# A hand-planned attention and long-convolution kernel: new starting rules for GpSimd, new due times for loads, and a new placement of the exponentials on VectorE

## The chip, the cores and the metric

The kernel runs on one core of a Trainium2 chip. The metric is the device time of one execution in microseconds (us), lower is better.

## The reference

```
x = A_q                                    # [1, 2048, 640], bf16
g = sigmoid((x * gate_w).sum(-1))          # one gate for each token
# A: a shift convolution of 4 taps along time, then a convolution of full length
k_shift[t] = sum_j A_k[t - j] * shift_k[:, j]
kv = k_shift * A_v
y  = irfft(rfft(pad(kv)) * rfft(pad(ssm_k)))[:2048] + kv * ssm_D
a  = x * y
# B: attention, 32 heads of 20 columns for the queries, one shared head for keys and values
q = (x @ wq) in 32 heads;  k = x @ wk;  v = x @ wv          # k, v: [2048, 20]
p = softmax(q @ k.T * 20 ** -0.5)          # 32 x 2048 x 2048
b = (p @ v, heads side by side) @ wo
out = g * a + (1 - g) * b
```

## The kernel before

**Attention is the main work.** The 32 heads by 2048 queries are cut into 32 groups of 4 heads (rows r = 0 to 3 of TensorE) by 512 queries, called G, and the 2048 keys into 16 steps, called j. One (G, j, r) is a tile of 128 keys by 512 queries, 2048 tiles in all. For each tile TensorE makes the scores in PSUM (`score`, L1310), an engine takes the exponential and writes bf16, and TensorE multiplies by the values and adds in PSUM bank 6 (`PVmm`, L1400). At a group's end VectorE copies the sums to `acc` (L1474), a round trip through DRAM (`den`, `rcp`, `rbc`) spreads the reciprocals of the sums, and GpSimd multiplies (`onorm`, L1486).

**Two engines take exponentials.** ScalarE takes most tiles, in units of alternately three tiles (ETA, 1536 columns) and two (ETB, 1024 columns). The table `DVE_J` lists for every group G the steps j in which two of the four tiles go to VectorE instead; this document calls such a two a pair. For a pair VectorE reads two banks of PSUM (dW, L1380, 512 columns each) and then runs three instructions of 1024 columns on SBUF alone (dX twice, L1392 and L1393, and ETd, L1395), a polynomial that gives the bits of the exponential.

**Side work fills the gaps.** The shift convolution (L1632), the long convolution as products with cosine and sine tables (`spectra` L1689, the complex product `mac` L1722 on GpSimd, `inverse` L1757), the projections of later queries (L1217) and the output projection (L1787) have priorities and run on TensorE where the attention leaves room. GpSimd's product of one chunk is five instructions; its inputs X and K have three buffers each. Fillers (L1843, L1848) are matmuls on zeros that keep TensorE busy.

**A planner in the kernel writes the order.** Every operation is an `Op` with an engine, dependencies, a priority and a cost in us. `Scheduler.run` always lets the engine with the earliest clock choose (`pick`), places the operation (`place`), and sets when its successors are ready from its planned end and a latency. A transfer's planned end comes from its bytes, the queue's planned rate and its `lat`. `emit` then writes each engine's list as it stands, with semaphore waits for the dependencies: each engine's order is fixed, and an engine waits where the plan was too early. `port=True` marks VectorE operations that the planner keeps apart from GpSimd's (`port_until`, `pool_until`); reads of PSUM, as dW, are not marked. `pool_may` decides whether GpSimd may begin at its time t, by what VectorE does then: x is the last operation placed on VectorE.

**The head and the loads.** `loads` fetches x in four blocks of 512 tokens (the first in two halves, called xnh), weights, and a slice of wq. `xT` transposes x on TensorE (L1075), with copies to SBUF on VectorE or ScalarE; `kproj` makes keys, values and the bound that the exponentials need; `qproj` projects the queries of groups 0 and 1 and sends a row `cr` of their norms by a small transfer (`qT<-cr`) into the queries, without which no score of that group can be made. `kshift` loads k with four transposing transfers (L1615) and v with four plain ones, on SyncE's queue, in which the q stores (`scr_q`), the q loads and `qT<-cr` stand too. `self.crow0` is the small transfer of group 0; the writer of `("qT0", 1, 4)` is that of group 1.

Of the kernel before, what the change touches and what calls it, by code (L numbers as in the profile page):

```python
# [37 lines left out]
OLD = 6.0  # L38
YOUNG = 4.0
WAITN = 0.5  # L40
HOLD = 0.1
IDLE = 0.3
WAITP = 6.0
PVB = 2
# [127 lines left out]
class Scheduler:  # L172
# [114 lines left out]
    def pool_may(self, t):  # L287
        d = self.order["dve"]
        if not d or not HOLD:
            return True  # L290
        x = d[-1]
        if not x.port and x.end > t + HOLD:
            return True
        if x.end <= t and not any(o.port and o.ready <= t + IDLE for o in self.cand["dve"]):
            return True
        w = [o.ready + (WAITP if o.name != "onorm" else WAITN) for o in self.cand["pool"] if o.ready <= t]
        return bool(w) and t > min(w)
# [175 lines left out]
    def place(self, op, e):  # L473
        t = self.t[e]
        op.eng = e
        if e == "pe":
            mode = MODE.get(op.name, "f")
            if mode != self.mode:
                t += SWITCH
                self.mode = mode  # L480
        if op.alts:
            for x in op.alts:
                self.cand[x].discard(op)
            op.fn, op.cost = op.alts[e]
        else:
            self.cand[e].discard(op)
        if op.main and e == "pe":
            for b in op.banks or ():
                if not self.bank_claimed[b]:
                    self.bank_claimed[b] = True  # L490
                    op.deps.update(self.bank_last[b])
        start = max(t, op.ready)
        if op.kind == "d":
            if op.nbytes:
                begin = max(start + 0.1, self.dma_bw)
                self.dma_bw = begin + op.nbytes / 300e3
                op.end = max(self.dma_bw, start + op.iss) + op.lat
            else:
                op.end = start + op.iss + op.lat
            self.t[e] = start + op.iss  # L500
            best = min(range(NLANES), key=lambda l: self.lanes[l][-1].end if self.lanes[l] else -1.0)
            op.lane = best
            if self.lanes[best]:
                op.deps.add(self.lanes[best][-1])
            self.lanes[best].append(op)
            op.value = 16 * len(self.lanes[best])
        else:
            if op.port and e == "dve":
                op.end = max(start, self.pool_until - PORTP) + op.cost
                self.port_until = op.end  # L510
            elif e == "pool":
                op.end = max(start, self.port_until - PORTD) + op.cost
                self.pool_until = op.end
            else:
                op.end = start + op.cost
            self.t[e] = op.end
        op.start = start
        op.placed = True
        if e == "pe" and op.cost > 0.05:
            self.active.append((op.end - op.cost * 0.92, op.end))  # L520
        if e == "pe":
            if op.name != "qk":
                self.rows = set()
            elif op.cont:
                self.rows.add(op.row)
            else:
                self.rows = {op.row}
        if op.name in ("tp0", "tp1"):
            b = STAGES[int(op.name[2])][2]
            self.bank_claimed[b] = self.bank_busy[b] = False  # L530
            self.bank_last[b] = [op]
            self.bank_ready[b] = op.end + LATX
        if op.name == "pv":
            if op.stage is not None:
                self.filler = self.filler2[op.stage]
            self.can_fill = not op.last
            self.acc = None
        elif op.name == "acc":
            self.acc = op
        if e == "pool" and self.main_started and HOLD:  # L540
            d = self.order["dve"]
            if len(d) > 1 and d[-1].end > t and not d[-1].port:
                op.deps.add(d[-2])
        self.order[e].append(op)
        self.linear.append(op)
        gr = op.grp
        if gr is not None:
            if e == "pe" and op in gr.mms:
                gr.pos += 1
                if gr.pos == len(gr.mms) and self.open is gr:  # L550
                    self.open = None
            elif op in gr.evacs:
                if all(x.placed for x in gr.evacs):
                    b = gr.bank
                    self.bank_busy[b] = False
                    self.bank_last[b] = [gr.mms[-1]] + list(gr.evacs)
                    self.bank_ready[b] = max(x.end + (LATX if self.main_started else LATS[x.eng, "pe"]) for x in gr.evacs)
        for s in op.succ:
            s.nun -= 1
            lat = 0.0 if (s.eng == "pe" and e == "pe") else self.lat_of(op, e, s.eng)  # L560
            s.ready = max(s.ready, op.end + lat)
            sg = s.grp
            if sg is not None and s.eng == "pe" and not (op.grp is sg):
                sg.nun -= 1
                sg.ready = max(sg.ready, op.end + lat)
                if sg.nun == 0:
                    self.gcand.add(sg)
            if s.nun == 0:
                self.enable(s)
# [73 lines left out]
NSC, NDC, NB = 16, 5, 4  # L643
# [16 lines left out]
PORTP = 0.05  # L660
PORTD = 0.14
PORTW = 0.2
INB = ()
LASTG = 31
STAGES = ((0, 256, 6), (256, 128, 5), (384, 128, 6))
DVE_J = ((), (3,), (4, 6, 11, 14), (3, 8, 14), (1, 2, 5, 10), (7, 12, 13), (3, 11), (2, 9, 10, 12), (1, 4, 7, 11, 12, 14), (1, 12), (2, 4, 8, 10, 14), (2, 7, 11), (1, 6, 9, 13), (5, 8, 13, 14), (6, 8, 13), (1, 3, 10, 13, 14), (12,), (2, 9, 14), (2, 8, 9, 13), (1, 8, 9, 13), (2, 4, 6, 11, 12, 14), (1, 8, 11, 12), (), (1, 8, 11, 13, 14), (2, 6, 10, 13, 14), (7, 14), (1, 3, 6, 9, 12), (6, 11, 14), (4, 7, 12), (1, 7, 10), (1, 4, 6, 8, 10, 12, 14), (3, 5))
SCALE = float(DH) ** -0.5


# [32 lines left out]
class Kernel:  # L702
# [171 lines left out]
    def loads(self):  # L874
        T, aps = self.T, self.aps
        x = aps["A_q"][0].rearrange("(i p) d -> p i d", p=128)
        wq = aps["B_wq"].rearrange("(p dc) n -> p dc n", dc=NDC)
        for b in range(NB):
            for lo, hi in ((0, 2), (2, 4)) if b == 0 else ((0, 4),):
                xl = self.dma(T["xn"][:, 4 * b + lo:4 * b + hi, :], x[:, 4 * b + lo:4 * b + hi, :],  # L880
                              writes=[("xn", b) if b else ("xnh", lo)], nbytes=110000 * (hi - lo),
                              prio=-9 + b + 0.1 * lo, lat=6.0)
            if b == 0:
                self.dma(T["wq"][:, :, 0:80], wq[:, :, 0:80], writes=[("wqst", 0)], prio=-8.5, lat=5.0)
        self.xl = [xl]
        for n, w, pr in (("wkr", "B_wk", -98.8), ("wvr", "B_wv", -98.7)):
            self.dma(T[n][:, :, :], aps[w].rearrange("(p dc) c -> p dc c", dc=NDC), writes=[n], eng="act",
                     prio=pr, lat=4.5)
        self.dma(T["gwr"][:, :], aps["gate_w"].rearrange("(p dc) -> p dc", dc=NDC), writes=["gwr"],
                 eng="act", prio=-98.6, lat=5.5)  # L890
        self.dma(T["wq"][:, :, 80:640], wq[:, :, 80:640], writes=[("wqst", 1)], nbytes=716800, prio=-4,
                 after=self.xl)
        self.dve(lambda e: e.memset(T["Drow"][:, :], 0.0), (), ["Drow"], 0.4, prio=-990)
# [169 lines left out]
    def xT(self):  # L1063

        T = self.T
# [1 line left out]
        plan += [(b, 0, 4, d0, min(2, NDC - d0)) for b in range(1, NB - 1) for d0 in range(0, NDC, 2)]  # L1067
        plan += [(NB - 1, c, 1, 0, NDC) for c in range(4)]
        for b, c0, nc, d0, nd in plan:
            gr = self.group("xT", 0.5 + 0.1 * b, banks=(0, 1, 2, 3, 4, 5, 7))  # L1070
            n = 128 * nc
            for dc in range(d0, d0 + nd):
                for ci in range(nc):
# [531 lines left out]
    def kshift(self):  # L1605
# [4 lines left out]
        self.dma(T["wtap"][:, :, :], self.aps["A_shift_k"].rearrange("(c p) j -> p c j", p=128), writes=["wtap"],  # L1610
                 nbytes=5120, prio=3, after=self.crow0, lat=3.0)
        self.dve(lambda e: e.memset(T["kTr"][:, :, 12:16], 0.0), (), [("kTr", -1)], 0.2, prio=20, after=self.crow0)
        for b in range(NB):
            o, i = T["kTr"][:, :, 16 + 512 * b:528 + 512 * b], k[512 * b:512 * b + 512, :]
            x = self.g.add("sp", lambda e, o=o, i=i: e.dma_start_transpose(o, i), (), [("kTr", b)], 0.1, kind="d",  # L1615
                           nbytes=655360, prio=14 + b, lat=1.6, after=self.crow0, name="ld_k")
            x.iss = 3.3
            self.dma(T["kv"][:, 4 * b:4 * b + 4, :], v[:, 4 * b:4 * b + 4, :], writes=[("kvl", b)], nbytes=655360,
                     prio=14.5 + b, name="ld_v", after=self.crow0)
        sh = [128, NDC * 4, 128]  # L1620
        self.dve(lambda e: e.tensor_tensor(
            T["kdiag"][:, :, :, :].rearrange("p c j d -> p (c j) d"), T["ident"][:, :].unsqueeze(1).to_broadcast(sh),
# [280 lines left out]
```

## Time and profile before

| What | Value |
|---|---|
| median of three runs (lowest, highest) | 862.49 us (861.33, 862.59) |
| the profiled execution: its own time | 861.71 us |
| its span on the core, first to last instruction | 859.9 us |
| ScalarE busy | 841.7 us |
| VectorE busy | 788.3 us |
| TensorE busy (fillers among it) | 836.1 us |
| GpSimd busy | 378.1 us |
| first exponential of the attention begins at | 20.63 us |
| last one begins at | 852.98 us, takes 1.45 us |

The span is what the profile's times count from. Busy times are unions of an engine's instructions; a share of busy time says little by itself here, since TensorE runs fillers and VectorE's instructions include the time that they stand locked. Groups of instructions are given by line, engine and operation, as "out<-in", with their count, busy time, mean duration in ns of one, and the idle time of their engine just ahead of them. SPq is SyncE's queue. The chain of waits is read back from the last instruction: at each step what released it.

### The profile page before, as it was taken

The numbers are of one execution on the slowest core, as the hardware profiler recorded it, in microseconds if no ns is written. First come the engines' busy times: TensorE is split into PE (matmuls) and PEld (weight loads), VectorE is DVE, ScalarE is ACT, GpSimd is POOL, SyncE is SP. The second block draws the span as 40 slices with busy tenths as digits, with TensorE's granted clock in tenths as the row PEclk, the third lists the DMA queues.
The fourth block names the chain that finished last, engine by engine and source line by source line (L and its number), as shares of the span: only waits on it lengthen the run. The fifth ranks groups of instructions, "written<-read, shape, count | busy, mean of one in ns | idle before, by whom it ended". The sixth has DMA issues, their size and how long they took to land.

```text
span 859.9 us, 18774 instructions
## 1 busy us (share of the span) xinstructions
PE 836.1 (97%) x8073; PEld 349.3 (41%) x8073; DVE 788.3 (92%) x968; ACT 841.7 (98%) x753; POOL 378.1 (44%) x317
## 2 busy tenths in 40 slices
PE   8999999999999999999999999999999999999998
PEld 5244433443344444444334434444343344433334
DVE  7679999999989999999999989999999988889995
ACT  6989999999999999999999999999999999999997
POOL 3656104566444356553317754335666565000000
PEclk9999999999999999999999999999999999999999
DMA  6910130002110000100120101100200001312111
GB/s 177 270 55 8 39 87 22 14 13 52 47 44 20 14 8 27 38 20 20 31 60 14 45 21 42 30 14 14 44 20 21 15 2 45 82 31 64 39 38 40
DMA packets 55765, 36.31 MB, mean 42 GB/s; under 512 B 33057, under 2 KB 51714, under 8 KB 55682
## 3 DMA queue, kind: packets, MB, share of 16 engines
q1 hardware_dynamic: 55106, 34.90, 15.0%
q8 instruction: 63, 1.03, 0.5%
q10 hardware_dynamic: 576, 0.22, 0.1%
q14 instruction: 20, 0.16, 0.1%
HBM read 20.31 MB, written 8.51 MB: 34 GB/s over the span
## 4 chain that ended last, share of the span: by engine, by line
ACT 78%; PE 17%; DVE 4%; DMA 0%; issue 0%; POOL 0%; POOLq 0%
ACT ETA L1347 47%; ACT ETB L1347 32%; PE ps L1310 5%; PE ps L1689 3%; PE ps L1400 3%; PE ps L1757 2%; PE ps L1843 1%; PE ps L1848 1%; DVE dW L1380 1%; DVE dX L1392 1%; PE ps L1511 1%; PE ps L1217 1%; DVE dX L1393 1%; PE ps L1075 0%; DMA qT<-cr 0%; DVE ETd L1395 0%
## 5 line engine op out<-in xcount | busy, mean ns | idle before, releaser
L1347 ACT ACTIVATE ETA<-ps 128x1536 bf16<-128x1536 f32 x366 | 579.6, 1584 | 5.6 <-PE ps L1310 5.4
L1347 ACT ACTIVATE ETB<-ps 128x1024 bf16<-128x1024 f32 x365 | 424.5, 1163 | 0.0
L1310 PE MATMUL ps<-qT,kT 32*128 32x512 bf16 (+2 forms) x2176 | 302.9, 372 | 14.6 <-ACT ETA L1347 7.2
L1722 POOL TENSOR_TENSOR Pp<-X,K 128x1024 f32<-128x1024 bf16 (+1 forms) x80 | 145.3, 1824 | 140.6 <-DVE K L1710 42.3
L1380 DVE TENSOR_SCALAR dW<-ps 128x512 f32<-128x512 f32 x220 | 149.7, 681 | 32.8 <-PE ps L1310 32.3
L1310 PEld LDWEIGHTS ps<-qT,kT 32*128 32x128 bf16 x2176 | 77.9, 91 | 238.1 <-ACT ETB L1347 110.1
L1392 DVE SCALAR_TENSOR_TENSOR dX<-dW 128x1024 f32<-128x1024 uint16 x110 | 165.5, 1505 | 1.6
L1395 DVE SCALAR_TENSOR_TENSOR ETd<-dX,dW 128x1024 int16<-128x1024 f32 x110 | 163.5, 1486 | 0.3
L1393 DVE SCALAR_TENSOR_TENSOR dX<-dX,dW 128x1024 f32<-128x1024 f32 x110 | 159.8, 1452 | 0.8
L1400 PE MATMUL ps<-ETA,vaug 128*32 128x512 bf16 (+2 forms) x1174 | 153.9, 372 | 0.3 <-DVE acc L1474 0.3
L1400 PE MATMUL ps<-ETB,vaug 128*32 128x512 bf16 (+2 forms) x778 | 146.7, 373 | 0.1
L1722 POOL TENSOR_TENSOR AB<-Pp 128x256 bf16<-128x256 f32 x80 | 67.7, 846 | 83.6 <-DVE dX L1393 32.0
L1689 PE MATMUL ps<-ssm_kT,Tcs 128*128 128x256 bf16 x600 | 91.7, 276 | 0.3
L1757 PE MATMUL ps<-AB,Tcs 128*128 128x256 bf16 x600 | 88.9, 274 | 0.0
L1689 PE MATMUL ps<-kv,Tcs 128*128 128x256 bf16 x600 | 87.6, 275 | 0.1
L1722 POOL TENSOR_TENSOR Pp<-Pp 128x512 f32<-128x512 f32 x40 | 57.0, 1425 | 51.2 <-DVE dX L1393 20.3
L1843 PE MATMUL ps<-Tcs,zeros 128*32 128x512 bf16 (+1 forms) x900 | 74.0, 383 | 1.0 <-DVE acc L1474 0.9
L1689 PEld LDWEIGHTS ps<-ssm_kT,Tcs 128*128 128x128 bf16 x600 | 50.7, 98 | 38.7 <-issue 28.1
L1757 PEld LDWEIGHTS ps<-AB,Tcs 128*128 128x128 bf16 x600 | 51.1, 98 | 33.6 <-issue 26.4
L1689 PEld LDWEIGHTS ps<-kv,Tcs 128*128 128x128 bf16 x600 | 49.9, 98 | 35.3 <-issue 24.5
L1486 POOL TENSOR_TENSOR oT<-acc,rbc 128x512 bf16<-128x512 f32 x7 | 10.3, 1476 | 110.9 <-DMA rbc<-scr_d 88.4
L1486 POOL TENSOR_TENSOR oTn<-acc,rbc 128x512 bf16<-128x512 f32 x24 | 42.9, 1787 | 36.4 <-DVE ETd L1395 21.5
(148 smaller groups left out, 629.3 us busy)
## 6 DMA issues: line engine op xcount, KB each, us to landing
rbc<-scr_d SPq DMA_DIRECT2D x31, 256.0 KB
scr_o<-oTn SPq DMA_DIRECT2D x24, 128.0 KB
kv<-in_A_v_dram SPq DMA_DIRECT2D x4, 640.0 KB
out_dram<-outsb SPq DMA_DIRECT2D x15, 160.0 KB
xn<-in_A_q_dram SPq DMA_DIRECT2D x3, 640.0 KB
scr_q<-xT SPq DMA_DIRECT2D x15, 128.0 KB
qT<-scr_q SPq DMA_DIRECT2D x12, 160.0 KB
oTp<-scr_o SPq DMA_DIRECT2D x12, 160.0 KB
```

Source lines behind the costliest of these rows:

```text
L1310: return e.matmul(self.bank(bk, n, n * t), T["kT4"][32 * r:32 * r + 32, 128 * jt:128 * jt + 128], T[k][32 * r:32 * r + 32, g, q0:q0 + n], ...
L1347: op("act", lambda e: e.activation(et(n)[:, 0:w], self.ps[:, lo:lo + w], ACT.Exp, scale=SCALE), [("ps", base[n % 2] + k) for k in range(le ...
L1380: self.evac(gr, "dve", lambda e, bk, c=c: e.tensor_scalar(W[:, c], self.bank(bk), SCALE * LOG2E * 128.0, 128.0 * (127 - KDN) - 32768.0, AL ...
L1392: V(lambda e: e.scalar_tensor_tensor(X[:, :], w, DP, w, ALU.add, ALU.mult), [kW], ["dX"], c_dve(1024), **k)
L1393: V(lambda e: e.scalar_tensor_tensor(X[:, :], X[:, :], DQ, w, ALU.add, ALU.mult), [kW], ["dX"], c_dve(1024), **k)
L1395: V(lambda e: e.scalar_tensor_tensor(E, X[:, :], DA, W[:, :], ALU.mult, ALU.add), [kW, "dX"], [("ETd", pe)], c_dve(1024), **k)
L1400: return op("pe", lambda e: e.matmul(self.bank(b, n)[32 * r:32 * r + 32, :], T[va][:, j, :], src, start=(j == 0), stop=(j == NSC - 1), til ...
L1486: self.pool(lambda e: e.tensor_tensor(out, T["acc"][:, :], T["rbc"][:, :], ALU.mult), ["acc", "rbc"], [key], 1.27, prio=p, port=True, name ...
L1689: self.mm(gr, lambda e, bk, lhs=lhs, rhs=rhs, comp=comp, n=n: e.matmul(self.bank(bk, 256, 256 * comp), lhs, rhs, start=(n == 0), stop=(n = ...
L1722: f = lambda e: e.tensor_tensor(out, a, b, alu)
L1757: self.mm(gr, lambda e, bk, lhs=lhs, fc=fc, comp=comp, h=h: e.matmul(self.bank(bk, 256, 256 * h), lhs, AB[:, fc, :, comp, :], start=(fc == ...
L1843: sch.filler, *sch.filler2 = ([[lambda e, r=r, st=st, b=b, n=n: e.matmul(self.bank(b, n)[32 * r:32 * r + 32, :], self.T["zeros"][:, 0:32], ...
```

## The change

There are five edits. (1) `pool_may`: where the last VectorE operation is a read of PSUM still running, GpSimd begins only if what is left of it and the ready PSUM reads behind it come to at least `COVER` times the shortest GpSimd operation that is ready; where it is a marked operation that began after a gap of VectorE of over `BUBBLE`, GpSimd does not begin; `HOLD` goes from 0.1 to 0.05. (2) `place`: a GpSimd operation that was ready over `TIED` before it was placed gets a dependency on the last VectorE operation that has ended by plan, and so waits for it. (3) `loads` and `xT`: other values of `lat` for six kinds of transfer, and the transposes of the last block of x come ahead of those of the third in priority. (4) `kshift`: the fourth load of k and of v wait for the small transfer of group 1. (5) `DVE_J`: 113 pairs for 110. By fours of groups from 0 to 31 the pairs are 8, 13, 16, 16, 12, 15, 15, 15 before and 10, 13, 14, 15, 15, 14, 14, 18 after.

```diff
--- before.py
+++ after.py
@@ -38,7 +38,7 @@
 OLD = 6.0
 YOUNG = 4.0
 WAITN = 0.5
-HOLD = 0.1
+HOLD = 0.05
 IDLE = 0.3
 WAITP = 6.0
 PVB = 2
@@ -289,8 +289,13 @@
         if not d or not HOLD:
             return True
         x = d[-1]
+        if x.port and x.end > t and len(d) > 1 and x.start > d[-2].end + BUBBLE:
+            return False
         if not x.port and x.end > t + HOLD:
-            return True
+            c = min((o.cost for o in self.cand["pool"] if o.ready <= t), default=0.0)
+            free = x.end - t + sum(o.cost for o in self.cand["dve"] if not o.port and o.ready <= x.end)
+            if free >= COVER * c:
+                return True
         if x.end <= t and not any(o.port and o.ready <= t + IDLE for o in self.cand["dve"]):
             return True
         w = [o.ready + (WAITP if o.name != "onorm" else WAITN) for o in self.cand["pool"] if o.ready <= t]
@@ -541,6 +546,8 @@
             d = self.order["dve"]
             if len(d) > 1 and d[-1].end > t and not d[-1].port:
                 op.deps.add(d[-2])
+            elif len(d) > 1 and op.ready + TIED < t:
+                op.deps.add(d[-1] if d[-1].end <= t else d[-2])
         self.order[e].append(op)
         self.linear.append(op)
         gr = op.grp
@@ -660,10 +667,13 @@
 PORTP = 0.05
 PORTD = 0.14
 PORTW = 0.2
+COVER = 0.3
+TIED = 0.1
+BUBBLE = 0.04
 INB = ()
 LASTG = 31
 STAGES = ((0, 256, 6), (256, 128, 5), (384, 128, 6))
-DVE_J = ((), (3,), (4, 6, 11, 14), (3, 8, 14), (1, 2, 5, 10), (7, 12, 13), (3, 11), (2, 9, 10, 12), (1, 4, 7, 11, 12, 14), (1, 12), (2, 4, 8, 10, 14), (2, 7, 11), (1, 6, 9, 13), (5, 8, 13, 14), (6, 8, 13), (1, 3, 10, 13, 14), (12,), (2, 9, 14), (2, 8, 9, 13), (1, 8, 9, 13), (2, 4, 6, 11, 12, 14), (1, 8, 11, 12), (), (1, 8, 11, 13, 14), (2, 6, 10, 13, 14), (7, 14), (1, 3, 6, 9, 12), (6, 11, 14), (4, 7, 12), (1, 7, 10), (1, 4, 6, 8, 10, 12, 14), (3, 5))
+DVE_J = ((), (3, 9, 14), (2, 6, 10, 14), (4, 9, 14), (4, 11, 14), (2, 6, 11, 13), (2, 9), (5, 10, 11, 14), (1, 2, 3, 8, 12), (7, 13), (3, 7, 13, 14), (5, 9, 14), (1, 5, 9, 13), (1, 5, 9), (2, 5, 8, 12), (2, 6, 9, 11), (1, 11), (2, 5, 9, 11, 14), (1, 5, 8, 13), (3, 6, 11, 14), (2, 5, 9, 13), (1, 3, 10), (1, 13), (2, 5, 7, 9, 14), (5, 8, 14), (3, 7, 8, 11, 13), (2, 7, 8, 14), (6, 14), (4, 5, 7, 12), (3, 4, 6, 10), (1, 4, 6, 9, 12, 14), (1, 2, 4, 5))
 SCALE = float(DH) ** -0.5
 
 
@@ -879,15 +889,15 @@
             for lo, hi in ((0, 2), (2, 4)) if b == 0 else ((0, 4),):
                 xl = self.dma(T["xn"][:, 4 * b + lo:4 * b + hi, :], x[:, 4 * b + lo:4 * b + hi, :],
                               writes=[("xn", b) if b else ("xnh", lo)], nbytes=110000 * (hi - lo),
-                              prio=-9 + b + 0.1 * lo, lat=6.0)
+                              prio=-9 + b + 0.1 * lo, lat=6.3 if b else 3.9)
             if b == 0:
-                self.dma(T["wq"][:, :, 0:80], wq[:, :, 0:80], writes=[("wqst", 0)], prio=-8.5, lat=5.0)
+                self.dma(T["wq"][:, :, 0:80], wq[:, :, 0:80], writes=[("wqst", 0)], prio=-8.5, lat=5.9)
         self.xl = [xl]
         for n, w, pr in (("wkr", "B_wk", -98.8), ("wvr", "B_wv", -98.7)):
             self.dma(T[n][:, :, :], aps[w].rearrange("(p dc) c -> p dc c", dc=NDC), writes=[n], eng="act",
-                     prio=pr, lat=4.5)
+                     prio=pr, lat=3.7)
         self.dma(T["gwr"][:, :], aps["gate_w"].rearrange("(p dc) -> p dc", dc=NDC), writes=["gwr"],
-                 eng="act", prio=-98.6, lat=5.5)
+                 eng="act", prio=-98.6, lat=4.4)
         self.dma(T["wq"][:, :, 80:640], wq[:, :, 80:640], writes=[("wqst", 1)], nbytes=716800, prio=-4,
                  after=self.xl)
         self.dve(lambda e: e.memset(T["Drow"][:, :], 0.0), (), ["Drow"], 0.4, prio=-990)
@@ -1067,7 +1077,7 @@
         plan += [(b, 0, 4, d0, min(2, NDC - d0)) for b in range(1, NB - 1) for d0 in range(0, NDC, 2)]
         plan += [(NB - 1, c, 1, 0, NDC) for c in range(4)]
         for b, c0, nc, d0, nd in plan:
-            gr = self.group("xT", 0.5 + 0.1 * b, banks=(0, 1, 2, 3, 4, 5, 7))
+            gr = self.group("xT", 0.5 + 0.1 * b - (0.12 if b == NB - 1 else 0.0), banks=(0, 1, 2, 3, 4, 5, 7))
             n = 128 * nc
             for dc in range(d0, d0 + nd):
                 for ci in range(nc):
@@ -1610,13 +1620,16 @@
         self.dma(T["wtap"][:, :, :], self.aps["A_shift_k"].rearrange("(c p) j -> p c j", p=128), writes=["wtap"],
                  nbytes=5120, prio=3, after=self.crow0, lat=3.0)
         self.dve(lambda e: e.memset(T["kTr"][:, :, 12:16], 0.0), (), [("kTr", -1)], 0.2, prio=20, after=self.crow0)
+        w = self.g.writer
+        early = [w["qT0", 1, 4]]
         for b in range(NB):
+            late = self.crow0 + (early if b > 2 else [])
             o, i = T["kTr"][:, :, 16 + 512 * b:528 + 512 * b], k[512 * b:512 * b + 512, :]
             x = self.g.add("sp", lambda e, o=o, i=i: e.dma_start_transpose(o, i), (), [("kTr", b)], 0.1, kind="d",
-                           nbytes=655360, prio=14 + b, lat=1.6, after=self.crow0, name="ld_k")
+                           nbytes=655360, prio=14 + b, lat=1.6, after=late, name="ld_k")
             x.iss = 3.3
             self.dma(T["kv"][:, 4 * b:4 * b + 4, :], v[:, 4 * b:4 * b + 4, :], writes=[("kvl", b)], nbytes=655360,
-                     prio=14.5 + b, name="ld_v", after=self.crow0)
+                     prio=14.5 + b, name="ld_v", after=late)
         sh = [128, NDC * 4, 128]
         self.dve(lambda e: e.tensor_tensor(
             T["kdiag"][:, :, :, :].rearrange("p c j d -> p (c j) d"), T["ident"][:, :].unsqueeze(1).to_broadcast(sh),
```

## The prediction

> **What bounds the kernel now.** I read the page's busy shares first, then the cost groups, then ScalarE's waits, then the chain of waits around the waits found.
>
> ```profile
> PE 836.1 (97%) x8073; PEld 349.3 (41%) x8073; DVE 788.3 (92%) x968; ACT 841.7 (98%) x753; POOL 378.1 (44%) x317
> L1347 ACT ACTIVATE ETA<-ps 128x1536 bf16<-128x1536 f32 x366 | 579.6, 1584 | 5.6 <-PE ps L1310 5.4
> L1347 ACT ACTIVATE ETB<-ps 128x1024 bf16<-128x1024 f32 x365 | 424.5, 1163 | 0.0
> L1380 DVE TENSOR_SCALAR dW<-ps 128x512 f32<-128x512 f32 x220 | 149.7, 681 | 32.8 <-PE ps L1310 32.3
> L1392 DVE SCALAR_TENSOR_TENSOR dX<-dW 128x1024 f32<-128x1024 uint16 x110 | 165.5, 1505 | 1.6
> ```
>
> The bound is the row of exponentials on ScalarE: from 20.63 us (timeline) to about 854.4 it idles 5.3 us. In the chain, successive ETA start at 23.00, 25.26, 27.52: 2.26 us per five tiles, **0.452 us a tile**. TensorE at 97% is partly filler (L1843). VectorE computes the tiles that ScalarE is spared, at 92%.
>
> ScalarE's timeline shows where the 5.3 us are: before 45.14 (1.80), 48.84 (1.31), 382.40 (0.53), 500.31 and 503.64 (0.18 + 0.82), 795.98 (0.30), 821.31 (0.32). The exponential after such a gap takes 0.1 us longer (1.45 for 1.34). The chain around the first two, then SyncE's timeline:
>
> ```profile
> 38.98 0.49 DVE qT L1224
> 39.48 3.94 DMA qT<-cr
> 43.42 0.05 issue
> 43.47 0.38 PE ps L1310
> ...
> 46.44 1.82 PE ps L1632 x16
> 48.27 0.56 PE ps L1310 x2
> ```
>
> ```profile
> 33.42 0.59 SPq L725 DMA_DIRECT2D kv<-in_A_v_dram  x1
> 34.05 4.20 SPq L1615 DMA_TRANSPOSE kTr<-in_A_k_dram  x1
> 38.30 0.58 SPq L725 DMA_DIRECT2D kv<-in_A_v_dram  x1
> 38.93 0.50 SPq L725 DMA_DIRECT2D scr_q<-qT  x1
> 39.48 0.60 SPq L725 DMA_DIRECT2D qT<-cr  x1
> ```
>
> The row `cr` is ready at 36.47 (VectorE, 35.79 + 0.68), but SyncE is issuing the fourth transpose of k until 38.25, so the small transfer goes out at 39.48 and lands at 43.42. A score of group 1 stands at TensorE's head: 1.93 us idle. The clock record then shows half rate from 45.14 to 48.55, 3.41 us, in which TensorE cannot catch up: the second gap. The same record of half rate stands at 499.1, beside the gap at 503.64.
>
> The head, by its timeline:
>
> ```profile
> 2.73 5.80 PE L1848 MATMUL ps<-ident,zeros 128*128 128x512 bf16 x15 [2.73 <-DVE ident L909]
> 8.36 1.28 PE L1075 MATMUL ps<-ident,xn 128*128 128x128 bf16 x20
> 14.94 1.29 PE L1075 MATMUL ps<-ident,xn 128*128 128x128 bf16 x20
> 20.63 1.45 ACT L1347 ACTIVATE ETA<-ps 128x1536 bf16<-128x1536 f32 x1 [0.17 <-PE ps L1310]
> ```
>
> The trace's landing records have the two halves of the first x block at 4.11 and 5.15, the first slice of wq at 7.35, the other blocks at 9.13, 10.91 and 12.61. TensorE runs fillers until the first transposes at 8.14, and turns to the last block 2.3 us after it has landed.
>
> The last view is VectorE's groups in two windows, 740 to 842 (GpSimd has five instructions there) and 320 to 500:
>
> ```profile
> L1393 DVE SCALAR_TENSOR_TENSOR dX<-dX,dW 128x1024 f32<-128x1024 f32 x16 | 19.3, 1205 | 0.1
> L1393 DVE SCALAR_TENSOR_TENSOR dX<-dX,dW 128x1024 f32<-128x1024 f32 x26 | 41.0, 1576 | 0.1
> ```
>
> The same instruction takes 1.21 us without GpSimd beside it and 1.58 with it.
>
> [...] This trace agrees in the length of its two half-rate stretches (3.413 us); the busy share before them was low (1.47 of 3.40 us from 40.2; 1.86 of 3.50 from 494.5). [...] Here the fourth v load, issued at 38.30, has most of its landings at 42.7 to 43.1, and the small row lands just after it.
>
> **Part by part.** The sum is made against the profiled execution, 861.71 us: a span of 859.9 and 1.8 around it. It is 0.8 below the median of 862.49, which I add at the end.
>
> *Pairs.* 113 for 110: six tiles leave ScalarE, 6 x 0.452 = **2.7 us less**. This is the only part that lies on the bound itself. VectorE gains three times two dW reads (0.681) and three dX instructions: 3 x (1.36 + 3 x 1.21) = 15.0 us clean, 3 x (1.36 + 4.44) = 17.4 at today's means. It has 71.6 us idle (859.9 less 788.3), but unevenly. Groups 12 to 19 get 30 pairs for 28. Counting 0.452 us for each tile left on ScalarE, they run from about 334 to 540, and there VectorE is the fullest: 58.7, 59.1 and 58.9 of 60 us in the three stages from 320, 54.5 in that from 500; slack 6.7 us. Groups 28 to 31 get 18 for 15, where GpSimd is nearly idle.
>
> *GpSimd's gate and ties* (`pool_may`, `place`). No instruction is added; waits are. Today 110 x (1505 + 1452 + 1486 - 3 x 1213) ns = 88 us of VectorE are spent locked out. The new rule starts GpSimd only where running and ready PSUM reads cover 0.3 of the shortest instruction waiting, or by the old fallbacks, and adds a wait on a VectorE instruction when GpSimd was held over 0.1 us. Behind a waiting GpSimd instruction stand the rest of its five-instruction product, then the X and K buffers (three), then the spectra on TensorE and the inverse. GpSimd is busy 44%, and by its own waits it has room. On ScalarE's row I take this at nothing: the cover is VectorE's slack. Bounds: a gain of 2.1 us (all later gaps go) and a loss of 5. In 334 to 540, two pairs more at that stretch's mean need 2 x 6.0 = 12.1 us against 6.7 of slack; the lockouts there are 28 x 3 x 0.345 = 29 us, so a fall of a fifth pays for it. I expect such a fall, and put **1.0 us more** for new small gaps[...].
>
> *Fourth k and v loads* (`kshift`) wait for the row `cr` of group 1. SyncE is then free from 34.01, the row goes out at about 36.5 and lands behind the third v load (38.02 in the landing records), near 38.3. TensorE reaches the score at 41.5: no wait. Both gaps and their restarts go: 1.80 + 1.31 + 0.2 = **3.3 less**. Late next: the transpose (4.2 us of SyncE) and the v load go out from 38.3 to 43.2, and behind them the q stores and the q loads (46.90 today, perhaps 51). These are for group 2, due near 20.6 + 122 x 0.452 = 76. Hidden. If the planner puts a store or the score differently, it returns a part: bounds 0 and 3.3.
>
> *Head* (`loads`, `xT`). No transfer changes; due times do. For the first halves 0.85 + 0.73 + 3.9 = 5.5 and 6.2, for 7.6 and 8.3; for the last block 13.0 for 12.7, its transposes now ahead of the third's. The last transposes can start at 13.05 for 14.91: at most 1.9 us. VectorE and ScalarE have room (4.2 and 5.6 busy of 6.8 from 8.14 to 14.91) but must evacuate two blocks close together. I take **1.3 less**; bounds 1.9 less and 0.3 more. The projection's first slice of wq (7.35) is next in line.
>
> Sum: 861.7 - 2.7 - 3.3 - 1.3 + 1.0 = 855.4; at the median **856.2**.
>
> **Rivals.**
> *A: as summed*, 853 to 859.5. Chance 0.64.
> *B: the gate turns against VectorE.* A tied GpSimd instruction starts as a VectorE instruction ends, so it can catch the lock just ahead of the next dX, for its whole 1.2 to 2.1 us. For it: the rows with 1.58. Against: it now starts beside dW reads by preference. Its place is 334 to 540: with lockouts up by 15% VectorE is late by 12.1 + 4.4 - 6.7 = 9.8 us, in order-bound queues that hand it to TensorE and ScalarE, and I add 1.2 for the full stage at 620. 861.7 - 7.3 + 11 = 865.4, median 866. It is slower than before once the lockouts there rise by about a tenth. Chance 0.13.
> *C: loads and due times pay nothing.* The head is held by evacuations, and another late transfer takes the place of `cr`. Left is 861.7 - 2.7 + 0.7 = 859.7, median 860.5; 858.5 to 862. For it: x lands no earlier, and the queue still holds the same bytes. Chance 0.15.
> *D: every later gap goes too*: 861.7 - 2.7 - 5.3 - 0.7 - 1.9 = 851.1, median 852. [...] Chance 0.08.
>
> **Numbers.** 0.2% of 862.5 is 1.7 us, about what a measurement of this kernel can tell from no change: faster is below 860.8. A and D are faster whole (but for 0.01), C for about 0.09 of its 0.15: 0.80; same 0.08; slower 0.12, nearly all of B. 852.8 to 862 leaves out most of D and B.
>
> **What would show it.** ETA x365 and ETB x364; the first ETA near 19.3; dW x226; no gap near 45, no half rate there; the row `cr` ahead of the fourth transpose on SyncE; dX means below 1.45. Wrong if dX means rise, if VectorE is full from 334 to 540 and ScalarE shows gaps there, or if the first ETA stays at 20.6.

## The result and the profile after

The kernel after takes **855.42 us** (four runs, 855.23 to 858.1), the kernel before 862.54 beside it: a ratio of 0.9927 [0.9905, 0.9949]. The forecast was 856.2. The profiled execution of after is its slowest, 858.1 us, with a span of 856.3; a repeat of the same kernel (first experiment) has a span of 853.6. Where a step is checked, both profiles are used. The insertions shift line numbers: L1347 of before is L1357 in after, L1380 is L1390, L1392 is L1402, L1310 is L1320.

The page of after, engine totals and cost groups:

```profile
PE 832.3 (97%) x8045; PEld 347.7 (41%) x8045; DVE 790.2 (92%) x984; ACT 838.9 (98%) x750; POOL 382.8 (45%) x317
L1357 ACT ACTIVATE ETA<-ps 128x1536 bf16<-128x1536 f32 x365 | 564.5, 1547 | 3.4 <-PE ps L1320 3.1
L1390 DVE TENSOR_SCALAR dW<-ps 128x512 f32<-128x512 f32 x226 | 153.9, 681 | 22.3 <-PE ps L1320 21.5
L1402 DVE SCALAR_TENSOR_TENSOR dX<-dW 128x1024 f32<-128x1024 uint16 x113 | 160.6, 1422 | 1.6
```

Six tiles have gone over (dW x226 for x220), and VectorE is busy only 1.9 us longer than before, since a dX takes 1422 ns on the mean instead of 1505. ScalarE's wait ahead of ETA is 3.4 us, where it was 5.6. SyncE's timeline of after (start, duration, queue, line, transfer):

```profile
34.84 0.58 SPq L735 DMA_DIRECT2D kv<-in_A_v_dram  x1
...
39.17 0.62 SPq L735 DMA_DIRECT2D qT<-cr  x1
...
40.87 2.90 SPq L1628 DMA_TRANSPOSE kTr<-in_A_k_dram  x1
```

The row `cr` is now ahead of the fourth transpose, and from 20.9 to 413 us ScalarE has no gap over 0.11 us. The head of after, on TensorE:

```profile
3.00 4.45 PE L1861 MATMUL ps<-ident,zeros 128*128 128x512 bf16 x10 [3.00 <-DVE ident L919]
7.24 2.04 PE L1085 MATMUL ps<-ident,xn 128*128 128x128 bf16 x20
...
13.63 2.43 PE L1085 MATMUL ps<-ident,xn 128*128 128x128 bf16 x40
```

The last 40 transposes end at 16.06 (before: 16.23), and the first exponential begins at 20.92 here and at 19.91 in the repeat (before: 20.63). The head did not become shorter by the 1.3 us forecast.

Everything below uses one reckoning. From the timeline of a profiled execution the span falls into four parts: the **head** up to the first exponential, the **row** (from there to the end of the last one, less ScalarE's gaps), the **gaps**, and the **tail** after the last exponential.

| Kernel | median, us | head | row | gaps | tail | span |
|---|---|---|---|---|---|---|
| before | 862.5 | 20.63 | 828.37 | 5.43 | 5.46 | 859.9 |
| after | 855.42 | 20.92 | 826.26 | 3.66 | 5.45 | 856.3 |
| e1 after, repeated | 856.41 | 19.91 | 825.91 | 2.32 | 5.46 | 853.6 |
| e2 before + loads | 860.73 | 20.27 | 828.52 | 4.67 | 5.46 | 858.9 |
| e3 after - loads | 862.27 | 20.66 | 826.26 | 6.69 | 5.46 | 859.1 |
| e4 after - ties | 866.04 | 20.08 | 826.88 | 12.37 | 5.47 | 864.8 |
| e5 before + ties | 859.76 | 19.79 | 828.04 | 4.43 | 5.46 | 857.7 |
| e11 before + loads + ties | 858.40 | 21.00 | 827.95 | 4.97 | 5.46 | 859.4 |
| e9 after, 110 pairs | 861.54 | 20.11 | 828.02 | 2.12 | 9.14 | 859.4 |
| e10 after - gate - ties | 871.17 | 20.08 | 826.03 | 11.64 | 11.63 | 869.4 |
| e6 after, 4 fillers fewer | 855.41 | 18.82 | 825.97 | 3.22 | 5.46 | 853.5 |
| e12 e6 + holes filled | 853.04 | 19.02 | 825.61 | 1.23 | 5.47 | 851.3 |
| e7 after, no products | 853.77 | 20.07 | 824.90 | 2.77 | 5.47 | 853.2 |
| e8 before, 24 tiles less | 859.09 | 20.08 | 821.66 | 10.42 | 5.46 | 857.6 |

Before, run beside the experiments, had medians from 862.1 to 862.4. The profiled execution of e11 took 861.19 us, well over its median, so its row of the table is not compared with others. A row of the table is one profiled execution; a median is of several.

### The profile page after: what moved, and what is told of

Its sections match the earlier page's. It is cut to its first block, busy times and chain, and to the rows that moved or that the text cites. A ratio compares the mean times of both kernels' runs of the same rounds, so it can differ in the third digit from the quotient of the medians.

```text
span 856.3 us, 18753 instructions
## 1 busy us (share of the span) xinstructions
PE 832.3 (97%) x8045; PEld 347.7 (41%) x8045; DVE 790.2 (92%) x984; ACT 838.9 (98%) x750; POOL 382.8 (45%) x317
## 4 chain that ended last, share of the span: by engine, by line
ACT 60%; DVE 19%; PE 19%; issue 1%; DMA 0%; POOL 0%; POOLq 0%
ACT ETA L1357 36%; ACT ETB L1357 24%; PE ps L1320 5%; DVE ETd L1405 4%; DVE dX L1403 4%; DVE dW L1390 4%; DVE dX L1402 4%; PE ps L1770 3%; PE ps L1410 3%; PE ps L1702 3%; PE ps L1856 1%; PE ps L1861 1%; DVE X L1715 1%; PE ps L1800 0%; PE ps L1085 0%
## 5 line engine op out<-in xcount | busy, mean ns | idle before, releaser
L1357 ACT ACTIVATE ETA<-ps 128x1536 bf16<-128x1536 f32 x365 | 564.5, 1547 | 3.4 <-PE ps L1320 3.1
L1357 ACT ACTIVATE ETB<-ps 128x1024 bf16<-128x1024 f32 x364 | 409.8, 1126 | 0.5 <-PE ps L1320 0.2
L1320 PE MATMUL ps<-qT,kT 32*128 32x512 bf16 (+2 forms) x2176 | 301.0, 372 | 10.9 <-ACT ETA L1357 4.7
L1390 DVE TENSOR_SCALAR dW<-ps 128x512 f32<-128x512 f32 x226 | 153.9, 681 | 22.3 <-PE ps L1320 21.5
L1320 PEld LDWEIGHTS ps<-qT,kT 32*128 32x128 bf16 x2176 | 77.9, 91 | 229.0 <-ACT ETB L1357 109.7
L1402 DVE SCALAR_TENSOR_TENSOR dX<-dW 128x1024 f32<-128x1024 uint16 x113 | 160.6, 1422 | 1.6
L1410 PE MATMUL ps<-ETB,vaug 128*32 128x512 bf16 (+2 forms) x774 | 148.5, 373 | 1.3 <-ACT ETA L1357 0.8
L1735 POOL TENSOR_TENSOR AB<-Pp 128x256 bf16<-128x256 f32 x80 | 61.1, 764 | 102.6 <-DVE ETd L1405 34.6
L1735 POOL TENSOR_TENSOR Pp<-Pp 128x512 f32<-128x512 f32 x40 | 55.2, 1380 | 52.1 <-DVE dX L1403 20.3
L1856 PE MATMUL ps<-Tcs,zeros 128*32 128x512 bf16 (+2 forms) x876 | 72.8, 381 | 0.9 <-DVE acc L1484 0.7
L1496 POOL TENSOR_TENSOR oTn<-acc,rbc 128x512 bf16<-128x512 f32 x24 | 46.7, 1948 | 40.4 <-DVE xT L1234 23.1
```

Source lines behind the costliest of these rows:

```text
L1320: return e.matmul(self.bank(bk, n, n * t), T["kT4"][32 * r:32 * r + 32, 128 * jt:128 * jt + 128], T[k][32 * r:32 * r + 32, g, q0:q0 + n], ...
L1357: op("act", lambda e: e.activation(et(n)[:, 0:w], self.ps[:, lo:lo + w], ACT.Exp, scale=SCALE), [("ps", base[n % 2] + k) for k in range(le ...
L1390: self.evac(gr, "dve", lambda e, bk, c=c: e.tensor_scalar(W[:, c], self.bank(bk), SCALE * LOG2E * 128.0, 128.0 * (127 - KDN) - 32768.0, AL ...
L1402: V(lambda e: e.scalar_tensor_tensor(X[:, :], w, DP, w, ALU.add, ALU.mult), [kW], ["dX"], c_dve(1024), **k)
L1410: return op("pe", lambda e: e.matmul(self.bank(b, n)[32 * r:32 * r + 32, :], T[va][:, j, :], src, start=(j == 0), stop=(j == NSC - 1), til ...
L1496: self.pool(lambda e: e.tensor_tensor(out, T["acc"][:, :], T["rbc"][:, :], ALU.mult), ["acc", "rbc"], [key], 1.27, prio=p, port=True, name ...
```

## The experiments

**The repeat, and the loads alone (e1, e2, e3).** e1 is after as it stands. e2 puts only the `kshift` edit on before, e3 takes only it out of after:

```diff
+        w = self.g.writer
+        early = [w["qT0", 1, 4]]
...
+            late = self.crow0 + (early if b > 2 else [])
...
-                           nbytes=655360, prio=14 + b, lat=1.6, after=self.crow0, name="ld_k")
+                           nbytes=655360, prio=14 + b, lat=1.6, after=late, name="ld_k")
...
-                     prio=14.5 + b, name="ld_v", after=self.crow0)
+                     prio=14.5 + b, name="ld_v", after=late)
```

> The changed kernel itself, beside which the next three are read. Theory A (the sum of the prediction, with the head corrected from its trace: the first exponential stayed at 20.9): a ratio near 0.992 to the kernel before, some 855.4 us. If the slower of its executions shown (858.1, profiled) is due to the half-rate stretch at 469.6 to 476.4, a profile without such a stretch should have about 2.5 us less span and no gap of ScalarE near 473 to 477.

> The kernel before with the fourth k and v loads alone waiting for the row cr of group 1. The planner's order of the compute engines should stay as it was. Theory A: both gaps near 45 and 49 go, with the half-rate stretch between them: 3.3 us less, about 859.2. Rival C (another late transfer takes the place of cr): within 0.5 us of 862.5, with the gap still there before the score of group 1.

> The changed kernel with the fourth k and v loads free again. Theory A: the row cr goes out behind the fourth transpose and lands near 44 instead of 41.6; the score that needs it stands at TensorE's head near 41.4, so about 2 to 3 us are lost again, around 858. Rival C: no difference, within 0.5 us of the changed kernel.

Measured: e1 0.9943 [0.9924, 0.9962], e2 0.9984 [0.9978, 0.9991], e3 1.0008 [0.9997, 1.0018]. On before the edit brings 1.4 us, in after it brings 5.9 (862.27 less 856.41; the interval of e1 alone is 1.6 us either way). In e2 the gap at 45 is gone, and the chain of waits around a new one at 56.3 (2.06 us) reads:

```profile
46.25 0.69 DVE cr L1236
...
50.95 2.81 DMA qT<-cr
53.76 0.09 issue
53.85 0.37 PE ps L1310
```

The same kind of small transfer is late again, now with the rows of groups 2 to 7. SyncE issues these from 46.96 (before: from 50.88), so they come earlier than in before, but the plan has put a score of group 2 earlier still: scores for pairs run ahead of the exponentials, and here the rows are due near 52 us, not near 76. The row lands at 53.76, after that score has stood at TensorE's head for 1.39 us. Half rate follows from 54.2. In after's order no such wait stands there. In e3 the old wait is worse than in before (gaps of 3.39 and 1.00 us at 46.8 and 50.3), since the order around it is another one.

**The ties alone (e4, e5, e11).** e4 takes the tie rule out of after, e5 puts it on before, e11 puts ties and loads on before:

```diff
+            elif len(d) > 1 and op.ready + TIED < t:
+                op.deps.add(d[-1] if d[-1].end <= t else d[-2])
```

> The changed kernel without the added semaphore ties, its planned order unchanged. Theory A: ties cost and give nothing on ScalarE's row: within 1 us of the changed kernel, with dX means near 1.43 us as there. Rival B (ties make GpSimd catch the lock ahead of the next dX): dX means fall below 1.40 and the time falls by 1 us or more. A third view (ties keep GpSimd from running ahead of the plan): dX means rise towards 1.48 and new gaps appear, 1 to 3 us more.

> The kernel before with the semaphore ties alone, its planned order and its 110 pairs unchanged. Theory D (ties belong to the new gate: under the gate more GpSimd instructions are started by the fallbacks, with nothing that holds them to their place beside VectorE, and only there do ties matter): within 1 us of 862.1, the lockouts of dX near 88 us as before. Theory E (ties are worth their gain under any gate, since they let a dX go ahead of GpSimd's long product): 3 us or more less, with fewer gaps of ScalarE after 300 us.

> The kernel before with the two edits that leave its planned order alone, the wait of the fourth loads and the ties. If they add: 1.4 + 2.5 us less, about 858.3, with a gap left near 56 before the scores of group 2. If the two are one gain counted twice (both only shift the head's stalls): about 859.8. What the changed kernel has beyond this is the part of the new order: gate, table and due times.

Measured: e4 1.0040 [1.0027, 1.0052], e5 0.9974 [0.9964, 0.9983], e11 0.9962 [0.9948, 0.9976]. On before, the ties bring 2.5 us and add up with the loads. In after's order they are worth 9.6 us (866.04 less 856.41), and without them 20 gaps of over 0.1 us stand in ScalarE's row, where e1 has seven. Almost half of the gap time of e4 (5.4 of 12.4 us) stands in or just behind two stretches of half rate, at 389.7 and 478.4, so part of the 9.6 comes by way of the clock. How one arises is in e4's timeline from 324 us, across engines:

```profile
324.29 2.99 POOL L1733 TENSOR_TENSOR Pp<-X,K 128x1024 f32<-128x1024 bf16 x1
325.55 2.81 DVE L1403 SCALAR_TENSOR_TENSOR ETd<-dX,dW 128x1024 int16<-128x1024 f32 x1
328.28 0.47 DVE L1721 SCALAR_TENSOR_TENSOR K<-K,cols,ps 128x256 bf16<-128x256 bf16 x1
328.81 0.39 PE L1318 MATMUL ps<-qT,kT 32*128 32x512 bf16 x1 [1.43 <-DVE K L1721]
330.49 1.45 ACT L1355 ACTIVATE ETA<-ps 128x1536 bf16<-128x1536 f32 x1 [1.36 <-PE ps L1318]
```

GpSimd's product begins while a dX runs (323.93 to 325.3) and takes 2.99 us, where one at 315.88 took 2.12. ETd begins while the product runs and ends 1.08 us after it, so it takes 2.81 us instead of 1.21; the K behind it, which reads a bank of PSUM, is late; TensorE waits 1.43 us for this K with a score next in its list; ScalarE idles 1.36. With the tie, in the repeat of after:

```profile
322.30 1.21 DVE L1405 SCALAR_TENSOR_TENSOR ETd<-dX,dW 128x1024 int16<-128x1024 f32 x1
322.45 3.03 POOL L1735 TENSOR_TENSOR Pp<-X,K 128x1024 f32<-128x1024 bf16 x1 [1.49 <-DVE K L1721]
```

Here the product waited, by its tie, for the VectorE instruction ahead of ETd (a copy to K; GpSimd idled 1.49 us). ETd was first by 0.15 us and took 1.21, and it is GpSimd's product that is drawn out, to 3.03 us. The last section counts such cases in before and after. The sum of locked time hardly shows it. Counted as the excess over 1.213 us, the mean of those dX and ETd of before that have no GpSimd instruction beside them, dX and ETd lose 77.5 us in e4 and 74.6 in e1 (88.4 in before). What counts is which instruction is hit, and what stands behind it. One instance is followed here; that such instances make up the whole gain is not shown.

**The table and the gate (e9, e10).** e9 is after with the old `DVE_J`. e10 is after with the old `pool_may` and `HOLD`, and without the tie rule as well (the edit of e4 is in it, although the expectation says that the ties are kept); what ran is this:

```diff
-HOLD = 0.05
+HOLD = 0.1
-        if x.port and x.end > t and len(d) > 1 and x.start > d[-2].end + BUBBLE:
-            return False
...
-            c = min((o.cost for o in self.cand["pool"] if o.ready <= t), default=0.0)
-            free = x.end - t + sum(o.cost for o in self.cand["dve"] if not o.port and o.ready <= x.end)
-            if free >= COVER * c:
-                return True
+            return True
...
-            elif len(d) > 1 and op.ready + TIED < t:
-                op.deps.add(d[-1] if d[-1].end <= t else d[-2])
```

> The changed kernel with the old table of 110 pairs; the planner orders everything anew. Theory A (six tiles at 0.452 us on ScalarE's row): 2.7 us more than the changed kernel, about 858.8. Rival, after the trial with 24 tiles less (TensorE's fixed order takes over when ScalarE alone is relieved): with a new order for the old table the difference may be anything from 0 to 6 us; above 4 would say that the table's fit to the order counts, not the number of pairs.

> The changed kernel with the old gate for GpSimd (any running PSUM read, no cover asked, HOLD 0.1), ties, 113 pairs, loads and due times kept; the planner orders everything anew. Theory A (the gate buys some 8 us of VectorE's lockouts, which lie in slack): within 2 us of the changed kernel. Theory F (pairs and gate were fitted to each other, and VectorE is late for this table without the gate): gaps of ScalarE of 5 us or more in all, 860 or above.

Measured: e9 0.9995 [0.9987, 1.0003], e10 1.0101 [1.0086, 1.0117]. In e9 the row grows by 2.1 us over e1, which is the six tiles, and the tail by 3.7: VectorE still has side work of the output when the last exponential is done. In e10 a gap of 5.85 us stands at 847.7, where TensorE waits for an ETd, between whose two dX and itself VectorE takes up two `outsb` copies and idles, and the tail is 6.2 longer than in e1. Of the 15.8 us between the profiles of e10 and e1, 12.0 are this gap and the longer tail. With the loads edit in all four, the medians form a square (e2 lacks the head edit, the three others have it):

| | neither gate nor ties | both |
|---|---|---|
| 110 pairs, old table | 860.7 (e2) | 861.5 (e9) |
| 113 pairs, new table | 871.2 (e10) | 856.4 (e1) |

The table alone is a loss of 10.4 us. The rules alone bring nothing (0.8 us more, within the intervals of e2 and e9), and only together do they gain. As e10 differs from e4 by the gate, the gate is worth 5.1 us (871.17 less 866.04) in the new table without ties; with ties and the new table it was not taken out alone. In the old table with ties it costs: e9 differs from e11 by the gate and the head edit, and takes 3.1 us more (861.54 less 858.40), with a tail of 9.14 us for 5.46.

**How much lockouts and ScalarE still cost (e7, e8).** e7 is after with GpSimd's complex products replaced by memsets; the long convolution is left out. e8 is before with one tile's exponential left out in 24 of the ETA:

```diff
-            f = lambda e: e.tensor_tensor(out, a, b, alu)
+            f = lambda e: e.memset(out, 0.0)
```
```diff
+            v = w - 512 if n % 30 == 20 else w
-            op("act", lambda e: e.activation(et(n)[:, 0:w], self.ps[:, lo:lo + w], ACT.Exp, scale=SCALE),
+            op("act", lambda e: e.activation(et(n)[:, 0:v], self.ps[:, lo:lo + v], ACT.Exp, scale=SCALE),
```

> The changed kernel with GpSimd's five products of each chunk replaced by memsets of the same outputs, so the long convolution is left out of the result; order and waits unchanged. Theory A (VectorE's lockouts lie in its slack): dX means fall from 1.43 to about 1.22 us, some 70 us of VectorE go idle, and the time falls only by the later gaps of ScalarE, 1 to 2.5 us. Rival (lockouts lie on the path throughout): 5 us or more less.

> The kernel before with the exponential of one tile left out in 24 of ScalarE's three-tile instructions, one in every thirty units, nothing put in their place: those tiles' weights are stale. Theory A (ScalarE's row is the bound and TensorE and VectorE follow it): 24 x 0.427 = 10.2 us less. Rival (TensorE at 97% or VectorE at 92% take over at once, in their fixed order): less than half of it, 3 to 5 us.

Measured: e7 0.9897 [0.9882, 0.9911], e8 0.9959 [0.9947, 0.9970]. In e7 the excess of dX and ETd falls from 74.6 to 8.4 us, and the time by 2.6 only (856.41 less 853.77), although the memsets are also shorter than the products (a Pp of 1024 columns 0.95 us for 2.12, an AB 0.31 for 0.73). So 66 us of lockouts cost the changed kernel, in this order, no more than about 2.6. In e8, ScalarE is spared some 10 us (24 times the 0.42 us by which an ETA of three tiles, 1.34, is longer than an ETB of two, 0.92), and the time falls by 3.2. About half of the freed time stands as new gaps (10.42 us in all for 5.43), 9.1 us of them behind TensorE's scores, whose order is fixed and filled for the old pace; exponentials behind gaps also take longer (an ETA 1.45 us for 1.34). A tile taken from ScalarE did not pay in full where the order stayed. Where the order was written anew it paid in after (the row is 2.1 to 2.5 us shorter), but not in e10.

**The head (e6).** After, with four of the first ten fillers dropped from TensorE's list:

```diff
+        head = [o for o in self.order["pe"] if o.name == "fill"][:10]
+        for o in head[:4]:
+            self.order["pe"].remove(o)
+            self.linear.remove(o)
```

> The changed kernel with four of its first ten fillers (L1861) left out, all else in the same order. Theory A (the due times of the first x block are met by its landings at 4.0 and 5.4, but ten fillers at half rate, 0.43 us each, keep TensorE until 7.0 to 7.4): transposes begin near 5.5, the first exponential comes 0.7 to 1.3 us earlier than the 19.9 to 20.9 of the changed kernel, and the time falls by as much, to about 855.3. Rival (the head is held by the tables and copies on VectorE and ScalarE, or by the x landings): first exponential within 0.3 us of the range, no difference in time.

Measured: 0.9931 [0.9914, 0.9948], median 855.41, and in the profile the first exponential at 18.82. The head of e6 on TensorE:

```profile
2.73 2.74 PE L1867 MATMUL ps<-ident,zeros 128*128 128x512 bf16 x6 [2.73 <-DVE ident L925]
5.26 1.92 PE L1091 MATMUL ps<-ident,xn 128*128 128x128 bf16 x20
```

The first transposes start at 5.26 instead of 7.24 in after (6.97 in the repeat), and the last ones end at 13.96 instead of 16.06 (15.05). The planner counts 0.218 us for a filler, and in after ten took 4.45 us: they follow each other by 0.43 us ahead of 8.82, where the clock record begins at full rate, and by 0.21 behind it. The second half of x is due at 6.2 in the plan, and has landed at 5.35 by the landing records; the fillers held TensorE until 7.24. By medians the gain over e1 is 1.0 us, within the spread of the two; the first exponential is 1.09 us earlier than in e1's profile.

**The half rate (e12).** The question is whether half rate follows from the low busy share that stands ahead of it. e12 is e6 once more, and in the three places where the plan leaves TensorE idle for over 0.4 us behind a score for a pair (about 465, 591 and 644 us) that score is repeated into its own bank, 15 repeats in all, before VectorE reads it:

```diff
+            for _ in range(min(int(gap / 0.22), 5)):
+                f = Op("pe", q.fn, 0.216, "c", "again", 0.0)
+                ...
+                pe.insert(pe.index(b), f)
+            for v in q.grp.evacs:
+                v.deps.add(f)
```

> The kernel with four head fillers fewer, and 15 repeats of a score for a pair (the same matmul again into the same bank, before VectorE reads it) put where the plan leaves TensorE idle around 465 (7), 591 (2) and 644 us (6). Theory [...]: no half-rate record near 467 or 649 in the profile, the ScalarE gaps behind it (about 2 us at 471 to 476) gone, and the profiled span near 851.5 to 852.5, against 853.5 with four fillers fewer alone; ratio to before 0.991. Rival (the half rate has another cause, such as the work itself or a fixed time, and low busy share is its companion): a half-rate record stays near 467 or 649 and the ratio stays at 0.993. Rival 2: the repeats stand in the way of the scores behind them (up to 5 x 0.216 us at 465 and 644), and new ScalarE gaps of about 1 us appear there at full clock: 0.993 to 0.995.

Measured: **853.04 us** (four runs, 852.78 to 853.59), 0.9896 [0.9879, 0.9912], the fastest kernel here, with an interval that lies below e6's. TensorE around 465 us in e6, then one of ScalarE's gaps behind it:

```profile
464.83 0.40 PE L1326 MATMUL ps<-qT,kT 32*128 32x512 bf16 x4
...
465.58 0.39 PE L1326 MATMUL ps<-qT,kT 32*128 32x512 bf16 x2 [0.35 <-ACT ETB L1363]
466.92 0.39 PE L1326 MATMUL ps<-qT,kT 32*128 32x512 bf16 x3 [0.95 <-ACT ETA L1363]
...
471.23 1.45 ACT L1363 ACTIVATE ETA<-ps 128x1536 bf16<-128x1536 f32 x1 [0.94 <-PE ps L1326]
```

And in e12:

```profile
465.05 2.48 PE L1344 MATMUL ps<-qT,kT 32*128 32x512 bf16 x16
...
471.35 1.16 ACT L1381 ACTIVATE ETB<-ps 128x1024 bf16<-128x1024 f32 x1
```

The locked dX ahead of these holes takes 3.03 us in both. In e6 TensorE is busy for 2.0 of the 3.41 us ahead of 467.4; from there the clock record has half rate for 6.8 us, and 2.1 us of gaps stand at 471.2, 472.9 and 474.9. In e12 the scores and their repeats fill these 3.41 us, the record shows full rate from the head to 850 us, and the gaps are gone. Work that computes nothing new made the kernel faster, so the half rate there hung on the low busy share, which was not just its companion. The gaps make up 1.99 of the 2.14 us between the two spans. One profile without half rate could be luck, but the mean granted clock of every run is on record: it is 0.999 or 1.0 in all four runs of e12, and 0.996 or less in all six of e6. Nor do the holes by themselves make the gaps: e1 has the same holes near 464, but full rate there, and no gap of ScalarE of over 0.1 us between 413 and 651.

## Why the prediction was right, step by step

The total came out within 0.8 us. Pairs and the wait of the row `cr` were foreseen rightly in kind; the head brought less than forecast and the ties more than nothing, and that these balanced is luck.

*Pairs: right.* Forecast 2.7 less. The row is 2.1 shorter in after, 2.5 in e1, and 2.8 in e12, where few gaps lengthen the exponentials behind them (1.45 us for 1.34). e9 gives 2.1 back. The step said nothing of the tail: the table with its 18 pairs in groups 28 to 31 also keeps the tail at 5.46, where the old one under the new rules has 9.14.

*GpSimd's gate and ties: lockouts right, the ties wrong.* The term that failed is "On ScalarE's row I take this at nothing". The ties alone are worth 2.5 us on before (without the kshift edit) and 9.6 in after, by a mechanism that the prediction does not have: which of the two engines begins first (the ETd followed takes 2.81 us behind the product in e4, 1.21 ahead of it in e1). The part on lockouts held: from 334 to 540 us their excess fell from 26.3 to 20.6 us, 22%, for "a fall of a fifth". (VectorE's slack there was 8.1 us by the profile of before, 206 less 197.9 busy, not the 6.7 put together from whole stages.) The term of 1.0 for new small gaps was too small: before's gaps are gone, and new ones of 3.7 us (after) or 2.3 us (e1) stand elsewhere, mostly in and behind stretches of half rate. In sum this came out near the forecast, which left some 2 us of old gaps beside the new: luck again.

*Fourth k and v loads: right about the wait, wrong in what is late next.* Forecast 3.3. On before's order it is 1.4, since "due near 20.6 + 122 x 0.452 = 76. Hidden." was false: the rows of groups 2 to 7 are due near 52 in that order, and one comes late (e2). The prediction's own bound, that a score put differently "returns a part", is what happened. In after's order, which has no such wait, it is 5.9, beyond the bound of 3.3. There the row is ready only at 39.14 and goes out at 39.17, not at 36.5; it is in time because nothing stands ahead of it in the queue by then.

*Head: failed in size.* Forecast 1.3 less from the due times. The head is 0.3 longer in after's profile and 0.7 shorter in e1's. Over all profiles, the first exponential lies from 19.79 to 21.00 with before's head (mean of five 20.35) and from 19.91 to 20.92 with after's and all its fillers (mean of seven 20.26), which by itself tells no gain. But the first exponential follows the moment at which the clock becomes full: 8.82 us in after, 7.01 in e1, at the same due times. At like moments after's head is shorter: 20.11 (e9, full at 7.44) for 20.63 (before, 7.59), and 20.66 (e3, 8.60) for 21.00 (e11, 8.32). A straight line through each set puts it 0.4 to 0.5 us ahead, an estimate from these twelve profiles, so about a third of the forecast. This is the prediction's own sign of being wrong, "if the first ETA stays at 20.6"; its other signs came as it said. The bound behind it, "the last transposes can start at 13.05", took the fillers ahead to end when planned; e6 shows that they do not.

*The sum.* 862.3 for before, 1.4 less for the loads, 2.5 for the ties: 858.4, which e11 measured. The other 2.0 to 3.0 us down to after's two medians belong to gate, table and head together. The square of medians shows that gate, ties and table can't be priced apart, so this division holds only for the order of steps taken.

*The rivals.* B (a tied product catches the lock ahead of the next dX) is refuted: without ties the locked time rises (74.6 to 77.5 us) and the kernel takes 9.6 us longer, and in the place followed it is the untied product that goes ahead (ETd 2.81 us), and the tie reverses it (1.21). C (loads and due times pay nothing) is wrong for the loads, and in the main right for the due times. D (every later gap goes) came true for the gaps that before had, but others stand in and behind stretches of half rate (2.1 us of them in e6); e12, at 853.0, shows that most of those can be planned away.

*Open.* The gate with ties kept and the table new was not run apart, nor was the head edit by itself. Not open is where the spread of after's runs comes from. In after and e1 together, the six runs with a mean granted clock of 0.997 or 0.998 take 855.0 to 855.6 us, the two at 0.995 and 0.996 take 858.1 and 857.3, and the two at 0.992 take 859.8 and 860.1: the spread goes with the half rate. Why one execution has more of it than another, no run shows.

## What to carry to other kernels

Where two engines exclude each other, don't sum the locked time (66 us of it cost no more than about 2.6 here): look at which instruction is hit and what waits behind it. A wait that lets the more urgent one start first can pay although it adds nothing but a wait (here 2.5 us on before, 9.6 in after). In a kernel whose order is written out, an edit's worth belongs to the order it stands in; undo it in the new kernel and do it alone in the old one before giving it a number. Where ScalarE idles, look some microseconds ahead for a stretch in which TensorE idles too, and try filling it: in e6 TensorE was busy for 2.0 of the 3.41 us ahead of half rate, and e12, which fills this and two other places, takes 2.4 us less by medians.

## What the runs showed of the hardware

**Half rate behind a low busy share.** In the 14 profiles, 19 stretches of half rate, 3.4 or 6.8 us long, lie between the head and 849 us (in before 3.413 us from 45.14 and from 499.11, in after 6.827 from 469.62). I laid windows of 3.413 us, the length of the shorter stretches, through each execution in step with its own stretches, and took TensorE's busy share of each. The windows directly ahead of the 19 had 0.16 to 0.67 (before 0.49 and 0.57, after 0.57). Of all other windows one had 0.66 (e3, just ahead of one with 0.36), the rest 0.69 or more (the lowest 0.79 in before, 0.70 in after). e9, e10 and e12 have no stretch, and their lowest windows, in step with the one after 850 us, have 0.74, 0.71 and 0.72. In the head, the clock is full at 8.82 us in one execution of the changed kernel and at 7.01 in another, and the first exponential follows 1.0 us apart (20.92 and 19.91).

**Which of two goes first.** In before and after, 280 dX and ETd took over 1.3 us. Each began behind a GpSimd instruction that was still running, and ended 1.07 to 1.09 us after that one. The 21 that began ahead of every GpSimd instruction beside them took 1.16 to 1.23 us, as did the 298 with none beside them. Where a GpSimd instruction began during a dX or ETd and outlasted it, and the next dX or ETd began 34 or 35 ns after that one's end, GpSimd went first: in all 20 such places, 13 in before and 7 in after. In before, a product begins at 266.78 under a dX of 1.22 us and takes 3.03 us, and the ETd behind it, from 267.87, takes 3.03 us as well.
